# The first u and weight loads wait for relus of the opening

## The chip, the cores and the metric

The kernel runs on one core of a Trainium2 chip. Such a core has a matrix engine (TensorE, "PE" in the profile; its weight loads are "PEld"), a vector engine (VectorE, "DVE"), a scalar engine (ScalarE, "ACT"), a general engine (GpSimd, "POOL") and a fifth that mainly issues transfers (SyncE, "SP"). Each runs its own list of instructions in order, and waits on semaphores for the others. Sixteen DMA engines move data between the chip's main memory (DRAM) and the on-chip memory (SBUF); TensorE writes its results to PSUM. The metric is the device time of one execution, in microseconds; lower is better.

## The reference

Two stages follow each other, for a batch of 8 sequences of 3200 rows, with u and v 256 wide and z 64 wide:

```python
scores = scale * np.matmul(z, z.transpose(0, 2, 1))      # scale = 1 / S
attn = np.maximum(scores, 0.0) ** 2
out = np.matmul(attn, v)
x = u * out
...
wq = x @ w_q
wk = x @ w_k
W_tok = scale * np.einsum('bsd,btd->bst', wq, wk)
mixed = np.einsum('bst,btd->bsd', W_tok, x)
return np.maximum(mixed, 0.0) @ w_out
```

The first stage is most of the work: for each sequence a 3200 x 3200 matrix of scores, relu and square of it, and its product with v.

## The kernel before

**Tiles.** Rows are cut into 25 tiles of 128. The 25 tiles are put into seven groups for the output side, six of 4 tiles and one of 1. For each batch b, group gi and tile ti there is one 128 x 512 block of squared scores, and blocks are made two at a time, as a *pair*. A pair goes through four steps: TensorE makes the scores into a PSUM tile (`sc`, line 224; two such PSUM slots exist, so the scores of pair p wait for the relu of pair p-2), VectorE or ScalarE takes the relu (`g`, lines 247 and 243), GpSimd or ScalarE squares it into fp16 (`at`, lines 262 and 260), and TensorE uses the square as the stationary operand against v (`acc`, line 303). Since the matrix is symmetric, some blocks are not made again but turned by a DMA transpose on SyncE (`tt`, `ttl`, line 282). When a group's accumulators are closed, `gate` adds their two halves (`both`, lines 319 and 320) and multiplies by u (`x_sb`, line 335, on GpSimd). The second stage's matmuls (`qk`, `hd`, `mx`, `fo`) are put in between the first stage's.

**A written-out order.** The program does not leave the order to a scheduler. A planner in the kernel keeps a clock for each engine (`clock`), one for SyncE (`sp_at`) and one for the DMA engines (`dma_at`), adds an estimated duration for each instruction that it emits, and decides by these clocks what comes next on each engine. Transfers by SyncE are queued with `move(ready, due, issue, takes, fn)`; when TensorE's clock has passed `ready` and SyncE is free, `send` emits the one with the earliest `due`. The chip knows nothing of these clocks: it sees only the order of instructions on each engine, and the semaphores for the data that they share.

**The opening.** Before the loop, z of batch 0 comes in four chunks (`load_first_z`: three by SyncE, one by ScalarE), is cast to fp16 and doubled (`cast_first`, by VectorE, ScalarE and GpSimd) and turned by TensorE (`turn_first`, line 126). v of batch 0 comes in five loads, issued by GpSimd between its casts and converted to fp16 on the way (`load_first_v`, line 108): tiles 0-1, 2-3, 12-17, 18-24, 4-11. TensorE's first product with v is that of tiles 2 and 3. In the plan, `v_at` holds the time at which each tile of v is taken to be there. Then stand, as moves of SyncE, the first load of u (`load_u(0, 0)`, line 853, needed by the first gate), the second (`load_u(0, 1)`, from `group_begun`), and seven weight loads (`load_weights`, line 184; w_out first).

The plan sends the first u load when its clock for TensorE stands at 10.2, the second at 15.2, w_out at 18.1. On the chip these three read only inputs and write fresh buffers, so in the program before they have nothing to wait for.

The function `use_pair` (line 583) emits one pair's scores and relu; `first_stage` (line 239) emits the relu itself. The relu of pair p is done by VectorE for pairs 0, 3, 4, 6, 7, 9 and by ScalarE for pairs 1, 2, 5, 8.

Of the kernel before, what the change touches and what calls it, by code (L numbers as in the profile page):

```python
# [16 lines left out]
def kernel(  # L17
# [10 lines left out]
    nc = tc.nc  # L28
# [58 lines left out]
    zT, vs, us, xs, xTs, qks, ks, hacc, hx, hss, rts, zds = ({} for _ in range(12))  # L87

    def rows(t, b):
        return t[b].rearrange("(p n) d -> p n d", n=NT)  # L90
# [31 lines left out]
    def turn_first(c):  # L122
        n0, nn = ZCH[c]
        tp = acc_tile(1 - c // 2, c % 2, "ztp", FP16)
        for i in range(nn):
            nc.tensor.transpose(
                tp[:, ts(i, P)], zd0[:, n0 + i, :, :].rearrange("p a k -> p (a k)"), ident
            )
        clock[PE] += 0.14 * nn
        ready = clock[PE] + FROM_PE  # L130
        on_act = max(clock[ACT], ready) < max(clock[DVE], ready)
        copy = nc.scalar.copy if on_act else nc.vector.tensor_copy
        copy(out=zT[0][:, ds(n0 * P, nn * P)], in_=tp[:, 0 : nn * P])
        z_at[c] = give(ACT if on_act else DVE, ready, 0.2 + 0.065 * nn)
# [26 lines left out]
    def load_u(b, gi):  # L161
        n0, nn = starts[gi] // P, widths[gi] // P
        us[b, gi] = pu.tile([P, 4, D], FP32, tag="u_sb", name="u_sb")
        nc.sync.dma_start(out=us[b, gi][:, 0:nn, :], in_=rows(u, b)[:, n0 : n0 + nn, :])

# [7 lines left out]
    def load_weights():  # L175
        wo32[0] = px.tile([P, ND, D], FP32, tag="x_sb", name="wo32")
        loads = [(wo32[0][:], moe_w_out.rearrange("(c p) e -> p c e", p=P))]
        for r in range(2):
            for w32, w in ((wq32, moe_w_q), (wk32, moe_w_k)):
                loads.append((w32[top(r), :, :], w.rearrange("(c p) h -> p c h", p=dh)))  # L180
        for half in range(2):
            loads.append((wk2[:, :, half, :], moe_w_k.rearrange("(c p) h -> p c h", p=P)))
        for i, (t, w) in enumerate(loads):
            move(18.0 + i, 26.0 + i, 0.65, 0.5, lambda t=t, w=w: nc.sync.dma_start(out=t, in_=w))
# [34 lines left out]
    def scores(p):  # L219
        assert len(ztimes) >= 5 * tiles[2 * p + 1][0] and p_chunk(p) in z_at, (p, clock, len(ztimes), z_at)  # L220
        sc = ps_tile("sc")
        for h, (b, gi, ti) in enumerate(tiles[2 * p : 2 * p + 2]):
            gs, gw = starts[gi], widths[gi]
            nc.tensor.matmul(  # L224
                out=sc[:, h, 0:gw],
                lhsT=zT[b][top(h), ts(ti, P)],
                rhs=zT[b][top(h), ds(gs, gw)],
                start=True,
                stop=True,
            )  # L230
        return sc

    def pieces(p):
        ws = [widths[gi] for _, gi, _ in tiles[2 * p : 2 * p + 2]]
        if ws[0] == ws[1]:
            return [(slice(0, 2), ws[0])]
        return [(slice(h, h + 1), w) for h, w in enumerate(ws)]

    def first_stage(p, sc, on_act):
        g = pg.tile([P, 2, W], FP32, tag="g", name="g")  # L240
        for hs, w in pieces(p):
            if on_act:
                nc.scalar.activation(  # L243
                    out=g[:, hs, 0:w], in_=sc[:, hs, 0:w], func=RELU, scale=GSCALE
                )
            else:
                nc.vector.tensor_scalar(  # L247
                    out=g[:, hs, 0:w], in0=sc[:, hs, 0:w], scalar1=0.0,
                    scalar2=GSCALE, op0=AOP.max, op1=AOP.mult,
                )  # L250
        return g

    def second_stage(p, g, on_act):
        at = pat.tile([P, 2 * W], FP16, tag="at", name="at")
# [264 lines left out]
    PE, DVE, ACT, POOL = range(4)  # L519
    clock = [0.0] * 4  # L520
    FROM_PE, HOP = 0.27, 0.12

    def give(engine, ready, weight):
        clock[engine] = max(clock[engine], ready) + weight
        return clock[engine] + HOP
# [9 lines left out]
    sp_at, dma_at = [0.0], [0.0]  # L535
# [4 lines left out]
    def at_time(t, fn):  # L540
        later.append((t, fn))

    def move(ready, due, issue, takes, fn, landed=None, may=None):
        moves.append((ready, due, issue, takes, fn, landed, may))

    def send(x):
        moves.remove(x)
        _, _, issue, takes, fn, landed, _ = x
        fn()
        begun = max(sp_at[0], clock[PE])  # L550
        dma_at[0] = max(dma_at[0], begun) + takes
        sp_at[0] = max(begun + issue, dma_at[0] - RING)
        if landed:
            landed(max(sp_at[0], dma_at[0]) + LANDS)
# [5 lines left out]
    def flush():  # L560
        while True:
            ripe = [x for x in later if x[0] <= clock[PE]]
            if not ripe:
                break
            x = min(ripe, key=lambda x: x[0])
            later.remove(x)
            x[1]()
        while sp_at[0] <= clock[PE] + 0.4:
            ripe = [x for x in moves if x[0] <= clock[PE] and (not x[6] or x[6]())]
            if not ripe:  # L570
                break
            send(min(ripe, key=lambda x: x[1]))

    def open_slot():
        clock[PE] = max(clock[PE], slots.pop(0))

    def close_slot(t):
        slots.append(t)

    def cold():  # L580
        return 2.0 if clock[PE] < 11.0 else 1.0

    def use_pair():
        open_slot()
        p = produced[0]
        produced[0] += 1
        sc = scores(p)
        clock[PE] += 0.22 * cold()
        ready = clock[PE] + FROM_PE
        on_act = max(clock[ACT], ready) + BIAS < max(clock[DVE], ready)  # L590
        done = give(ACT, ready, 1.03) if on_act else give(DVE, ready, 1.2)
        g = first_stage(p, sc, on_act)
        close_slot(done)
        pending.append((done, p, g))

# [108 lines left out]
    def batch_begun(b, t):  # L704
        if b + 1 < B:
            t += 6 if b == 0 else 0
            at_time(t + 6, lambda: (load_z(b + 1), push(3.0)))
            for half in range(2):
                at_time(
                    t + 18 + 3 * half,  # L710
                    lambda half=half: (double_z(b + 1, half), give(DVE, clock[PE], 0.98)),
                )
            for i in range(5):
                move(t + 24 + 6 * i, t + 40 + 6 * i, 1.28, 1.05, lambda i=i: turn_z(b + 1, i))
            for i in range(5):
                at_time(t + 20 + 13 * i, lambda i=i: (load_v(b + 1, 5 * i, 5), push(2.5)))

    def group_begun(b, gi, t):
        if gi == 0:
            batch_begun(b, t)  # L720
        if gi + 1 < NG:
            move(max(t + 2, clock[POOL] + SLACK), t + 7, 0.55, 1.6, lambda: load_u(b, gi + 1))
        elif b + 1 < B:
            move(max(t + 2, clock[POOL] + SLACK), t + 7, 0.55, 1.6, lambda: load_u(b + 1, 0))
# [113 lines left out]
    load_first_v(18, 7)  # L838
    load_first_v(4, 8)
    clock[:] = [4.5, 4.95, 4.7, 7.8]  # L840
    v_at = [4.5] * 2 + [8.2] * 2 + [18.7] * 8 + [11.2] * 6 + [14.7] * 7
    dma_at[0] = 16.0
    turn_first(0)
    cast_first(3, [1])
    give(DVE, 0.0, 0.65)
# [1 line left out]
    current.update(b=0, gi=0, left=list(range(NT)), fresh=True)  # L847
    groups.pop(0)
    use_pair()
    use_pair()  # L850
    turn_first(2)
    turn_first(3)
    move(10.0, 14.0, 0.55, 1.6, lambda: load_u(0, 0))
    load_weights()
    at_time(38.0, cast_weights)
    group_begun(0, 0, 12.0)

    total = B * sum(NT * (w // P) for w in widths)
    done_acc = 0
# [2 lines left out]
    while groups or work or current["left"]:  # L862
# [14 lines left out]
        p = produced[0]  # L877
# [21 lines left out]
    while extras or later or moves:  # L899
        x = next((x for x in extras if x[1] == "proj"), None)  # L900
        if not x:
            ripe = [x for x in moves if not x[6] or x[6]()]
            x = min(later + extras + ripe, key=lambda x: x[0])
        clock[PE] = max(clock[PE], x[0])
        if x in later:
            later.remove(x)
            x[1]()
        elif x in moves:
            send(x)
        else:  # L910
            extras.remove(x)
            x[2]()
# [74 lines left out]
```

## Time and profile before

| | |
|---|---|
| time, median of 3 runs | 791.21 us (791.0 to 795.83) |
| the profiled execution | 790.96 us, of which the span from first to last instruction is 789.2 us |
| TensorE clock granted, mean over the span | 0.994 |
| PE, POOL, ACT, DVE busy | 97%, 78%, 70%, 61% of the span |
| HBM read and written | 59.64 MB, 26.21 MB |
| DMA rate, mean | 181 GB/s |
| u loads | 48 of 512 KB, 8 of 128 KB |
| v loads | 35 of 320 KB, and the five of the opening |

How to read the lines that follow: a line of the timeline has the start and the length of some instructions in microseconds from the span's start, the engine, the line in the code, the operation, what it writes and reads, a count, and in brackets how long the engine was idle before it and what ended that. An engine's name with a q (SPq) means its instruction queue: issuing and waiting, not computing. A line of the chain of waits has start, length and what the end of the program was waiting for in that stretch. A line of stretches has the busy time and the count of instructions of each engine in a window, then the share of the full TensorE clock that was granted, the mean busy share of the DMA engines, and GB/s.

### The profile page before, as it was taken

What the parts mean: (1) busy time and instruction counts of PE and PEld (TensorE: products, weight loads), DVE (VectorE), ACT (ScalarE), POOL (GpSimd) and SP (SyncE); (2) the same over time, 40 slices, a digit from 0 to 9 for tenths busy, and PEclk for the clock granted to TensorE, in tenths of its full rate; (3) what the DMA queues carried; (4) which work ended last, traced back from release to release, by engine and by line L of the source; (5) the groups of instructions that cost most, each with busy time, mean ns of one, the idle gap of its engine ahead of it and who ended that gap; (6) DMA issues with size and microseconds to landing.
All of it is one profiled execution on the core that took longest, in us unless ns stands there. A gap on an engine that the chain in (4) does not pass through costs nothing.

```text
span 789.2 us, 28159 instructions
## 1 busy us (share of the span) xinstructions
PE 763.2 (97%) x12373; PEld 645.7 (82%) x12373; DVE 479.4 (61%) x479; ACT 551.8 (70%) x659; POOL 612.9 (78%) x418
## 2 busy tenths in 40 slices
PE   6989999999999999999999999999999999999976
PEld 5879898887888888888788887988788888888864
DVE  5755577664685656754587635666468654675634
ACT  5766478766776677786687678866778767777624
POOL 7887799886998769877798876888789775787830
PEclk9999999999999999999999999999999999999998
DMA  7999999999999979999999999999999998899425
GB/s 192 146 172 165 177 160 179 156 225 194 204 184 189 220 164 194 152 189 216 210 162 170 187 214 199 177 151 208 193 207 165 178 225 160 183 163 194 122 56 220
DMA packets 310636, 142.57 MB, mean 181 GB/s; under 512 B 287985, under 2 KB 291953, under 8 KB 310513
## 3 DMA queue, kind: packets, MB, share of 16 engines
q1 hardware_dynamic: 303600, 124.60, 83.4%
q0 software_dynamic: 6768, 15.98, 14.8%
q8 instruction: 96, 1.57, 0.9%
q14 instruction: 28, 0.22, 0.1%
q10 hardware_dynamic: 144, 0.20, 0.1%
HBM read 59.64 MB, written 26.21 MB: 109 GB/s over the span
## 4 chain that ended last, share of the span: by engine, by line
PE 91%; DVE 3%; DMA 2%; issue 1%; ACT 1%; POOL 1%; SPq 0%; DVEq 0%; POOLq 0%; ACTq 0%
PE acc L303 66%; PE sc L224 12%; PE fo L456 6%; PE qk L366 3%; DVE g L247 2%; PE hd L393 1%; PE mx L429 1%; DVE both L320 1%; DMA v_sb<-in_v_dram 1%; DMA hx<-ha 1%; ACT both L319 1%; POOL x_sb L335 1%; DVE ha L410 0%; DMA z<-in_z_dram 0%; SPq L349 0%
## 5 line engine op out<-in xcount | busy, mean ns | idle before, releaser
L262 POOL TENSOR_TENSOR at<-g 128x1024 f16<-128x1024 f32 (+2 forms) x245 | 451.5, 1858 | 82.5 <-DVE g L247 66.5
L303 PE MATMUL acc<-v_sb,at 64*128 64x256 f16 x7312 | 499.1, 270 | 5.0 <-DVE both L320 2.5
L247 DVE TENSOR_SCALAR g<-sc 128x1024 f32<-128x1024 f32 (+2 forms) x309 | 363.9, 1197 | 153.0 <-PE sc L224 137.6
L303 PEld LDWEIGHTS <-at 64*128 64x128 f16 x7312 | 393.0, 94 | 66.8 <-issue 12.7
L260 ACT ACTIVATE at<-g 128x1024 f16<-128x1024 f32 x223 | 229.4, 1036 | 30.7 <-DVE g L247 27.2
L243 ACT ACTIVATE g<-sc 128x1024 f32<-128x1024 f32 (+1 forms) x159 | 159.2, 1003 | 60.5 <-PE sc L224 59.8
L335 POOL TENSOR_TENSOR x_sb<-both,u_sb 128x512 f16<-128x512 f32 (+1 forms) x112 | 134.4, 1207 | 64.4 <-DVE both L320 63.8
L224 PE MATMUL sc<-zT 64*128 64x512 f16 x920 | 180.2, 378 | 3.5 <-DVE g L247 3.1
L303 PE MATMUL acc<-v_sb,tt 64*128 64x256 f16 x2304 | 158.7, 269 | 0.0
L320 DVE TENSOR_TENSOR both<-acc,both 128x512 f32<-128x512 f32 (+1 forms) x104 | 69.1, 670 | 128.9 <-ACT both L319 128.4
L303 PEld LDWEIGHTS <-tt 64*128 64x128 f16 x2304 | 123.3, 94 | 11.6 <-issue 0.4
L319 ACT COPY both<-acc 128x512 f32<-128x512 f32 (+1 forms) x104 | 58.4, 566 | 65.5 <-PE acc L303 63.5
L224 PEld LDWEIGHTS <-zT 64*128 64x128 f16 x920 | 56.8, 94 | 17.6 <-issue 12.4
L484 ACT ACTIVATE fo<-fo 128x1024 f32<-128x1024 f32 (+2 forms) x50 | 44.9, 908 | 23.5 <-PE fo L456 22.1
L446 ACT ACTIVATE rt<-mx 128x1024 f16<-128x1024 f32 (+1 forms) x49 | 45.1, 931 | 22.1 <-PE mx L429 21.8
L456 PE MATMUL fo<-wo,rt 128*128 128x256 f16 x400 | 53.1, 276 | 1.2 <-ACT rt L444 0.6
L456 PEld LDWEIGHTS <-rt 128*128 128x128 f16 x400 | 35.4, 98 | 15.6 <-issue 9.6
L379 ACT CAST qk<-qk 128x512 f16<-128x512 f32 (+1 forms) x54 | 29.4, 544 | 21.6 <-PE qk L366 21.6
L366 PE MATMUL qk<-xT_sb,wqk 64*128 64x256 f16 (+1 forms) x404 | 32.2, 265 | 0.1
L366 PEld LDWEIGHTS <-wqk 64*128 64x128 f16 x416 | 22.8, 94 | 2.5 <-issue 0.5
L303 PE MATMUL acc<-v_sb,ttl 64*128 64x256 f16 x384 | 24.6, 269 | 0.0
L303 PEld LDWEIGHTS <-ttl 64*128 64x128 f16 x384 | 19.7, 94 | 3.5 <-issue 0.8
(42 smaller groups left out, 163.9 us busy)
## 6 DMA issues: line engine op xcount, KB each, us to landing
u_sb<-in_u_dram SPq DMA_DIRECT2D x48, 512.0 KB, 5.1
out_dram<-fo SPq DMA_DIRECT2D x45, 512.0 KB, 4.7
v_sb<-in_v_dram POOLq DMA_DIRECT2D x35, 320.0 KB, 6.0
zn<-in_z_dram POOLq DMA_DIRECT2D x7, 400.0 KB, 5.7
tt<-at SPq DMA_TRANSPOSE x144, 4.4
out_dram<-fo SPq DMA_DIRECT2D x6, 256.0 KB, 2.1
u_sb<-in_u_dram SPq DMA_DIRECT2D x8, 128.0 KB, 3.9
hx<-ha SPq DMA_DIRECT2D x16, 64.0 KB, 4.7
```

Source lines behind the costliest of these rows:

```text
L224: nc.tensor.matmul(out=sc[:, h, 0:gw], lhsT=zT[b][top(h), ts(ti, P)], rhs=zT[b][top(h), ds(gs, gw)], start=True, stop=True,)
L243: nc.scalar.activation(out=g[:, hs, 0:w], in_=sc[:, hs, 0:w], func=RELU, scale=GSCALE)
L247: nc.vector.tensor_scalar(out=g[:, hs, 0:w], in0=sc[:, hs, 0:w], scalar1=0.0, scalar2=GSCALE, op0=AOP.max, op1=AOP.mult,)
L260: nc.scalar.square(out=out, in_=g[:, hs, 0:w])
L262: nc.gpsimd.tensor_mul(out=out, in0=g[:, hs, 0:w], in1=g[:, hs, 0:w])
L303: nc.tensor.matmul(out=accs[half, r][:, ds((j % 2) * D, D)], lhsT=weights(b, gi, ti, j)[top(r), :], rhs=vs[b][top(r), ti, :], start=(first ...
L319: nc.scalar.copy(out=both[:, 0 : n * D], in_=accs[half, 0][:, 0 : n * D])
L320: nc.vector.tensor_add(out=both[:, 0 : n * D], in0=accs[half, 1][:, 0 : n * D], in1=both[:, 0 : n * D])
L335: nc.gpsimd.tensor_mul(out=xs[b, gi][:, 0:n, :, r, :].rearrange("p n c d -> p (n c) d"), in0=both[:, 0 : n * D].rearrange("p (m d) -> p m ...
L366: nc.tensor.matmul(out=ps[:, r, 0 : n * P], lhsT=wqk[top(r), c, :, :].rearrange("p t h -> p (t h)"), rhs=xTs[b, gi][top(r), 0:n, c, :], st ...
L446: nc.scalar.activation(out=out, in_=ps[:, 0:nr, 0 : ND * n * P], func=RELU)
L456: nc.tensor.matmul(out=banks[r][:, ds(j * D, D)], lhsT=flat[:, ds((dc * n + j) * P, P)], rhs=wo[:, dc, :], start=(dc == 0 and j == 0), sto ...
```

## The change

Two things are changed, both for the plan's first microseconds.

First, a load that SyncE sends while the planner's TensorE clock is below 32 is given one more dependency: it waits for the last relu that by the plan's clock is done at that time. Since `send` uses what the move's function returns, only functions that return their instruction take part: `load_u`, which now returns it, and the weight loads. The transposes return nothing and are as before.

Second, some of the plan's numbers are others: v is taken to land earlier (`v_at`), the DMA engines to be free at 13 rather than 16, the first u load is wanted from 13 on rather than 10, and the first group is counted as begun at 14 rather than 12, which also moves the planned times of the next batch's loads of z and v by 2.

```diff
     def load_u(b, gi):
...
-        nc.sync.dma_start(out=us[b, gi][:, 0:nn, :], in_=rows(u, b)[:, n0 : n0 + nn, :])
+        return nc.sync.dma_start(out=us[b, gi][:, 0:nn, :], in_=rows(u, b)[:, n0 : n0 + nn, :])
...
-                nc.scalar.activation(
+                relu = nc.scalar.activation(
                     out=g[:, hs, 0:w], in_=sc[:, hs, 0:w], func=RELU, scale=GSCALE
                 )
...
-        return g
+        return g, relu
...
+    SEES = mybir.DependencyInfo(mybir.DependencyClass.Sync, mybir.DependencyReason.DATA)
+    EARLY = 32.0
+    relus = []
+
     def send(x):
         moves.remove(x)
         _, _, issue, takes, fn, landed, _ = x
-        fn()
+        sent = fn()
+        if sent is not None and clock[PE] < EARLY:
+            name = [i.ins.name for t, i in relus if t <= clock[PE]][-1]
+            tc.add_manual_dep(sent.ins, name, SEES, reason="not before this relu")
         begun = max(sp_at[0], clock[PE])
...
-        g = first_stage(p, sc, on_act)
+        g, relu = first_stage(p, sc, on_act)
+        if clock[PE] < EARLY:
+            relus.append((done, relu))
...
-    v_at = [4.5] * 2 + [8.2] * 2 + [18.7] * 8 + [11.2] * 6 + [14.7] * 7
-    dma_at[0] = 16.0
+    v_at = [4.5] * 2 + [6.5] * 2 + [13.0] * 8 + [8.5] * 6 + [10.5] * 7
+    dma_at[0] = 13.0
...
-    move(10.0, 14.0, 0.55, 1.6, lambda: load_u(0, 0))
+    move(13.0, 17.0, 0.55, 1.6, lambda: load_u(0, 0))
...
-    group_begun(0, 0, 12.0)
+    group_begun(0, 0, 14.0)
```

In the built program the first u load waits for VectorE's relu of pair 4, the second for that of pair 7 and w_out for that of pair 9; the loads of w_q and w_k, which stand between transposes as before, wait for relus of pairs 10 to 19. SyncE's first 31 transfers are of the same kinds in the same order. On TensorE the order is the same through the first group, and differs from the second group on. Over the whole program GpSimd has 253 squares in place of 245, ScalarE 215 in place of 223.

More of the change, by code (lines that the diff above doesn't have):

```diff
@@ L246, in first_stage @@
             else:
-                nc.vector.tensor_scalar(
+                relu = nc.vector.tensor_scalar(
                     out=g[:, hs, 0:w], in0=sc[:, hs, 0:w], scalar1=0.0,
```

## The prediction

> **What bounds the kernel now.** I read the page first.
>
> ```profile
> span 789.2 us, 28159 instructions
> ...
> PE 763.2 (97%) x12373; PEld 645.7 (82%) x12373; DVE 479.4 (61%) x479; ACT 551.8 (70%) x659; POOL 612.9 (78%) x418
> ```
>
> TensorE is busy in all but 26 us of the span, so a change elsewhere pays only where it closes one of its gaps or keeps its clock up. Next, the chain of waits in order of time, which says where the first gap comes from:
>
> ```profile
> 0.74 2.94 DMA z<-in_z_dram
> ...
> 3.74 0.45 POOL zd L120
> 4.18 6.57 DMA v_sb<-in_v_dram
> 10.75 0.14 issue
> ```
>
> The second v load (rows 2 and 3, issued by GpSimd at 4.18) takes 6.57 us to land, and the chain runs through it. SyncE's own timeline shows what is beside it:
>
> ```profile
> 0.74 1.36 SPq L105 DMA_DIRECT2D z<-in_z_dram  x3
> 2.15 0.91 SPq L164 DMA_DIRECT2D u_sb<-in_u_dram  x2
> 3.10 0.43 SPq L184 DMA_DIRECT2D wo<-in_moe_w_out_dram  x1
> 19.15 1.35 SPq L282 DMA_TRANSPOSE tt<-at  x1
> ```
>
> Two u loads of 512 KB and w_out of 256 KB are sent by 3.53, in front of that v load, and SyncE then has nothing to do until 19.15. The stretches by DMA share and clock:
>
> ```profile
> 6.00:9.50 3.50, 2.81 (x23) 1.32 (x19) 2.37 (x4) 3.00 (x4) 2.33 (x4) 1.00 1.04 346
> 9.50:14.50 5.00, 3.62 (x34) 2.90 (x36) 2.68 (x3) 3.55 (x4) 4.46 (x3) 0.68 1.11 224
> ```
>
> ```profile
> 7.90:11.30 3.40, 1.65 (x20) 1.10 (x22) 3.05 (x4) 2.31 (x3) 3.39 (x5) 1.00 1.10 276
> 11.30:14.70 3.40, 3.40 (x32) 2.63 (x30) 1.22 (x1) 2.74 (x3) 2.86 (x2) 0.50 1.07 214
> 14.70:18.10 3.40, 3.40 (x58) 2.98 (x55) 2.35 (x2) 1.14 (x3) 2.16 (x2) 1.00 0.59 119
> ```
>
> The columns are busy time and instructions of PE, PEld, DVE, ACT, POOL, then granted clock, DMA share and GB/s. The DMA engines are full from 6 to 14.5, at 346 GB/s while u passes and 224 GB/s once v is alone. TensorE is busy 1.65 us of 3.40 in the stretch where it waits for v, and in the very next stretch its clock is granted at 0.50. The wait for v is thus paid twice: as idle time, and as half clock.
>
> **What the loads' new waits cost.** In the built program the first u load waits for the relu of pair 4, the second for that of pair 7, w_out for that of pair 9, all on VectorE. With today's trace these end at 13.26, 17.52 and 19.51:
>
> ```profile
> 7.13 0.43 DVE L120 CAST zd<-z 128x512 f16<-128x512 f32 x1 [1.56 <-DMA z<-in_z_dram]
> 7.48 1.22 DVE L247 TENSOR_SCALAR g<-sc 128x1024 f32<-128x1024 f32 x1
> ...
> 9.74 1.22 DVE L247 TENSOR_SCALAR g<-sc 128x1024 f32<-128x1024 f32 x1
> ...
> 12.04 1.22 DVE L247 TENSOR_SCALAR g<-sc 128x1024 f32<-128x1024 f32 x1 [1.08 <-PE sc L224]
> 15.17 2.35 DVE L247 TENSOR_SCALAR g<-sc 128x1024 f32<-128x1024 f32 x2 [1.91 <-PE sc L224]
> 18.29 1.22 DVE L247 TENSOR_SCALAR g<-sc 128x1024 f32<-128x1024 f32 x1 [0.77 <-PE sc L224]
> ```
>
> (The relu of pair 0 is the row at 7.48, pair 3 at 9.74, pair 4 at 12.04, pairs 6 and 7 at 15.17, pair 9 at 18.29.) Behind w_out on SyncE stands the first transpose, issued at 19.15 today; on that clock it would go at 19.51 + 0.43 = 19.94, 0.8 us late, and everything behind it by at most that. Who needs these things, and when:
>
> ```profile
> 27.99 1.27 POOL L335 TENSOR_TENSOR x_sb<-both,u_sb 128x512 f16<-128x512 f32 x1 [1.14 <-DVE both L320]
> ...
> 40.08 0.61 POOL L190 CAST wo<-wo 128x512 f16<-128x512 f32 x1
> ```
>
> ```profile
> 33.09 0.79 PE L303 MATMUL acc<-v_sb,tt 64*128 64x256 f16 x10
> ```
>
> u at 27.99, w_out at 40.08, the first turned block at 33.09. A u load issued at 13.3 that took the whole 6.57 us of the v load would land at 19.9, eight us early. I cost the waits at nothing; the cover is those eight us for u, and some seven for the transpose even if it needs 6 us to land. The small weight loads (w_q, w_k) stand where they stood, between transposes, and wait for relus that end before the transposes around them may go. If the cover went, the gate would hold the first accumulator and each us would be paid by TensorE in full.
>
> **What goes: the wait for v.** How soon v can land is not in this trace; the nearest landings are these:
>
> ```profile
> v_sb<-in_v_dram POOLq DMA_DIRECT2D x35, 320.0 KB, 6.0
> ...
> v_sb<-in_v_dram POOLq DMA_DIRECT2D x2, 128.0 KB, 6.5
> ...
> z<-in_z_dram SPq DMA_DIRECT2D x1, 224.0 KB, 3.1
> ```
>
> At best like z in the same microseconds: 4.18 + 3.1 = 7.3. At worst no sooner than now, 10.75; later than now has no cause, as nothing new moves at that time. I take it near the z row, because what is removed (1.25 MB) is most of what the DMA engines carry between 6 and 9.5. Next in line behind v is then ScalarE, which makes the weights for these matmuls:
>
> ```profile
> 6.76 1.02 ACT L243 ACTIVATE g<-sc 128x1024 f32<-128x1024 f32 x1 [0.17 <-PE sc L224]
> 7.82 1.06 ACT L260 ACTIVATE at<-g 128x1024 f16<-128x1024 f32 x1
> 9.18 1.02 ACT L243 ACTIVATE g<-sc 128x1024 f32<-128x1024 f32 x1 [0.30 <-PE sc L224]
> ```
>
> The square of pair 1 ends at 8.88, so any v before that gives the same. The last z chunk, which shares the queue with u, should land earlier as well (the DVE cast at 7.13 waited 1.56 us for it), so the relu of pair 0 and the scores of pairs 2 and 3 move up by about 0.7 us, ahead of ScalarE's next relu. TensorE's first matmuls on v then start at 8.9 in place of 10.88. After eight of them (0.44) it needs a PSUM slot that the relu of pair 2 frees: 8.88 + 1.02 = 9.90. So it goes on at 9.95 where it now goes on at 11.33.
>
> ```profile
> 10.88 0.69 PE L303 MATMUL acc<-v_sb,at 64*128 64x256 f16 x8 [1.53 <-DMA v_sb<-in_v_dram]
> ...
> 18.21 0.40 PE L224 MATMUL sc<-zT 64*128 64x512 f16 x2
> ```
>
> Between these two rows TensorE's timeline lists six pairs of scores (12 matmuls) and 72 further acc matmuls, in the same order in both programs; the order differs only from the second group on, near 30 us. At full clock their rates are in the chain's rows:
>
> ```profile
> 15.56 0.22 PE sc L224 x2
> 15.78 0.98 PE acc L303 x18
> ```
>
> 6 x 0.22 + 72 x 0.98/18 = 5.24 us. Today this takes 18.21 - 11.33 = 6.88; the 1.64 us between is half of the 3.4 us at clock 0.50. Started at 9.95 and with the clock up, the work that now begins at 18.21 begins at 15.2: 3.0 us earlier, 1.4 from the start and 1.6 from the clock. The supply of relus and squares must keep pace: stepped through with 1.22 (DVE), 1.02 and 1.06 (ACT), the slots come free 0.15 to 0.2 us before TensorE asks. (The relu of pair 3 ends near 10.1; ScalarE then squares it and does the relu of pair 5, to 12.2, and TensorE wants that slot at 9.95 + 2.41 = 12.36.) That is thin; I take 0.2 off and count **2.8 us**.
>
> [...]
>
> **What moves: everything after 30 us.** The planner's clocks start with other numbers, so its order of scores, squares and transposes changes through all later batches, with no aim. What that can be worth is bounded by the idle time there is:
>
> ```profile
> 28.00:60.00 32.00, 29.29 (x476) 26.76 (x477) 19.34 (x20) 20.74 (x25) 28.51 (x23) 1.00 1.14 166
> ```
>
> ```profile
> 60.00:160.00 100.00, 98.76 (x1661) 89.93 (x1659) 66.07 (x65) 71.43 (x86) 81.87 (x55) 1.00 1.10 172
> ...
> 660.00:760.00 100.00, 100.00 (x1685) 84.83 (x1681) 57.17 (x58) 67.98 (x84) 74.30 (x46) 1.00 0.73 149
> sum 700.00, PE 695.70 PEld 591.74 DVE 431.31 ACT 500.42 POOL 560.83; mean PE 99.39 PEld 84.53 DVE 61.62 ACT 71.49 POOL 80.12
> ```
>
> TensorE is idle 2.71 us from 28 to 60, and in the seven windows of 100 us from 60 on between 1.24 (the first) and 0.00 (the last), 4.3 in all. A fresh draw of seven such windows scatters by about 0.36 x 2.6 = 0.9 us (0.36 is the spread of even chances between 0 and 1.24); with the first stretch I allow 2 us either way and take zero.
>
> **The sum.** The profiled execution took 790.96 us, a span of 789.2 and 1.8 around it; the median of three runs, 791.21, is 0.25 above it. 790.96 - 2.8 + 0.25 = **788.4**, with 786.4 to 790.4 as its own range.
>
> **The rivals.**
>
> *v is late for its own sake* (18%). The 6.57 us may be the time from GpSimd's issue to the first bytes rather than queueing behind u; the 35 later v loads take 6.0 with no u burst in front. At half of 346 GB/s, 128 KB need 0.76 us, alone 0.38, so the removal would give 0.4 us: 790.8. For it: the 6.0 row. Against: those loads are 2.5 times larger and run beside transposes and stores. [...]
>
> *The half-clock stretch stays* (10%). A wait for the slot from 9.4 to 9.9, or a thin supply, still leaves TensorE idle enough; only the 1.4 us of the earlier start remain: 790.96 - 1.4 + 0.25 = 789.8. For it: 1.65 of 3.40 busy was enough to halve the clock; against: with the earlier start that stretch would be busy some 2.8.
>
> *The new order stalls* (14%). The worst spot today is a run of scores at the end of the third group, waiting for relus:
>
> ```profile
> 52.60 0.39 PE L224 MATMUL sc<-zT 64*128 64x512 f16 x2 [0.30 <-DVE g L247]
> ...
> 54.38 0.39 PE L224 MATMUL sc<-zT 64*128 64x512 f16 x2 [0.79 <-DVE g L247]
> ```
>
> Two of its stalls come to 1.09 us. If the new order sets up three such spots more than the old one, the 2.8 us are gone; with five, one in most batches, the time is 788.4 + 5.45 = 793.9, slower than before. For it: eight squares move from ScalarE to GpSimd, so the new order is not a copy. Against: after 60 us no window has more than 1.24 idle.
>
> **Chances and range.** 58% for the forecast. The range of 785.8 to 792.0 takes in its own range with a little more, the first two rivals, and the edge of the third; about 2 in 10 is left out. About 1% (7.9 us) is what a measurement of this kernel can tell from no change. Faster by that would need 5 us beyond the opening, more than the 4.3 us of idle time between 60 and 760: 2%. Slower by that takes ten bad spots, a quarter of the third rival: 4%. Within: 94%.
>
> **What would show it.** Right, if in the new trace no DMA from SyncE but z stands before about 11, the second v load lands before 8.9, the chain passes through ScalarE's relu and square there, the stretch at clock 0.50 between 11 and 15 is gone and the first gate on GpSimd starts near 25.2 rather than 27.99. Wrong, if v still lands after 10 us, if the half clock shows later, or if the first gate is early and the end is not: then the order behind it took it back, and TensorE's idle time by windows of 100 us would show where. If u lands after the gate wants it, the cover was wrong.

## The result, and the profile after

The changed kernel takes 798.9 us (median of 16 runs, 793.21 to 809.85); the kernel before, run beside it, takes 792.81 us (16 runs, 790.86 to 795.83). The ratio is 1.0073, with a 95% interval of 1.005 to 1.0095: slower by 0.7%, where 788.4 us had been forecast. Ratios, and the figures of the runs further down, leave out executions that took over 1.5% longer than the fastest of the same kernel (here one of the 16, at 809.85 us). The profiled execution took 800.08 us, a span of 798.3.

The page of the kernel after; its first lines, and the chain by engine and by line:

```profile
span 798.3 us, 28144 instructions
...
PE 769.0 (96%) x12373; PEld 642.0 (80%) x12373; DVE 472.6 (59%) x478; ACT 548.1 (69%) x652; POOL 624.4 (78%) x426
...
PE 87%; DMA 5%; DVE 2%; ACT 2%; issue 1%; POOL 1%; SPq 0%; POOLq 0%; DVEq 0%; ACTq 0%
```

The same line of the chain in the kernel before:

```profile
PE 91%; DVE 3%; DMA 2%; issue 1%; ACT 1%; POOL 1%; SPq 0%; DVEq 0%; POOLq 0%; ACTq 0%
```

TensorE does the same 12373 matmuls, is busy 5.8 us longer with them, and the DMA engines' share of the chain is 5% where it was 2%.

The opening did what it was meant to do. SyncE's and TensorE's timelines of the kernel after (start, length, engine and line, operation, what it writes and reads, count):

```profile
0.74 1.34 SPq L105 DMA_DIRECT2D z<-in_z_dram  x3
11.85 3.45 SPq L164 DMA_DIRECT2D u_sb<-in_u_dram  x2
16.96 0.39 SPq L184 DMA_DIRECT2D wo<-in_moe_w_out_dram  x1
17.40 1.44 SPq L282 DMA_TRANSPOSE tt<-at  x1
```

```profile
7.42 1.03 PE L126 MATMUL ztp<-ident,zd 128*128 128x128 f16 x8 [0.26 <-POOL zd L120]
8.39 1.04 PE L224 MATMUL sc<-zT 64*128 64x512 f16 x4
9.22 0.91 PE L303 MATMUL acc<-v_sb,at 64*128 64x256 f16 x8
...
15.64 0.40 PE L224 MATMUL sc<-zT 64*128 64x512 f16 x2
...
18.52 1.05 PE L303 MATMUL acc<-v_sb,at 64*128 64x256 f16 x16 [0.31 <-DMA v_sb<-in_v_dram]
```

The first u load goes at 11.85 instead of 2.15, the first product with v is at 9.22 instead of 10.88, with no wait before it, and the scores that were at 18.21 are at 15.64. The first transpose is not late but earlier (17.40; it was at 19.15). The stretches of the opening, with the granted clock as the last figure but two:

```profile
7.90:11.30 3.40, 3.27 (x31) 1.76 (x30) 3.12 (x5) 2.15 (x3) 3.39 (x3) 1.00 0.98 166
11.30:14.70 3.40, 3.40 (x62) 3.09 (x58) 2.63 (x3) 2.71 (x4) 3.40 (x3) 1.00 1.05 196
```

TensorE is busy 3.27 us of the stretch in which it was busy 1.65, and the next is granted in full instead of at 0.50: 62 instructions pass in it, where 32 did.

So the time was lost later. The sum row over the same seven stretches of 100 us from 60 to 760:

```profile
sum 700.00, PE 688.11 PEld 575.06 DVE 417.19 ACT 492.58 POOL 568.73; mean PE 98.30 PEld 82.15 DVE 59.60 ACT 70.37 POOL 81.25
```

TensorE is idle 11.9 us there, against 4.3 before. Setting the n-th TensorE instruction of both traces side by side shows where, in these two executions: from the 1600th to the 5200th the kernel after is 2.3 to 3.4 us ahead; by the 5600th it is 2.1 us behind, and from the 10400th to the 10800th it falls from 1.4 to 9.1 us behind. In this execution, then, two places make the whole loss, 4.8 and 7.7 us, less the 3 us that it was ahead.

The later one first. ScalarE's, TensorE's and SyncE's timelines there, and the stretches around it:

```profile
656.13 0.84 ACT L260 ACTIVATE at<-g 128x128 f16<-128x128 f32 x2
662.85 0.38 ACT L484 ACTIVATE fo<-fo 128x256 f32<-128x256 f32 x1 [5.88 <-DMA out_dram<-fo]
663.93 1.02 ACT L446 ACTIVATE rt<-mx 128x1024 f16<-128x1024 f32 x1 [0.70 <-PE mx L429]
```

```profile
663.29 0.61 PE L429 MATMUL mx<-qk,hs 64*128 64x256 f16 x4 [4.71 <-ACT fo L484]
```

```profile
653.50 0.53 SPq L485 DMA_DIRECT2D out_dram<-fo  x1
```

```profile
653.50 9.27 DMA out_dram<-fo
```

```profile
655.00:658.50 3.50, 3.50 (x56) 2.75 (x53) 1.46 (x3) 1.97 (x4) 2.39 (x2) 1.00 1.09 254
658.50:661.80 3.30, 0.07 (x2) 0.00 (x0) 0.65 (x1) 0.00 (x0) 1.89 (x1) 1.00 1.60 152
661.80:668.60 6.80, 5.31 (x48) 4.03 (x47) 1.22 (x1) 1.99 (x3) 1.23 (x1) 0.50 0.74 210
668.60:672.00 3.40, 3.40 (x52) 2.68 (x52) 1.23 (x1) 1.02 (x1) 1.18 (x2) 1.00 0.61 137
```

The output tile `fo` has two buffers. ScalarE is to write the small output of the seventh group into the one whose store was issued at 653.50, and that store takes 9.27 us (the fourth fence, the chain of waits; the median of such stores is 4.4). For the 5.88 us before that write ScalarE does no relu, no square and frees no PSUM slot; TensorE stands 4.71 us; and then its clock is granted at 0.50 for 6.8 us, in which 48 instructions pass where the next 3.4 us let 52 through. (The DMA share counts a packet's whole time in the stretch in which it starts, so it can exceed 1.) The wait is paid a second time, as in the opening of the kernel before.

The earlier place is of the same kind, on VectorE:

```profile
318.17 1.00 DVE L410 TENSOR_TENSOR ha<-ha 128x256 f32<-128x256 f32 x1
...
331.08 0.43 DVE L420 TENSOR_TENSOR hs<-ha,hx 128x256 f16<-128x256 f32 x1 [3.22 <-DMA hx<-ha]
331.42 2.35 DVE L247 TENSOR_SCALAR g<-sc 128x1024 f32<-128x1024 f32 x2
```

```profile
315.64 8.30 SPq L282 DMA_TRANSPOSE tt<-at  x3
324.04 1.97 SPq L415 DMA_DIRECT2D hx<-ha  x2
```

```profile
332.69 0.39 PE L224 MATMUL sc<-zT 64*128 64x512 f16 x2 [1.38 <-DVE g L247]
...
333.82 0.40 PE L429 MATMUL mx<-qk,hs 64*128 64x256 f16 x4 [0.63 <-DVE g L247]
```

```profile
331.00:334.10 3.10, 1.09 (x16) 0.60 (x14) 2.69 (x3) 0.30 (x1) 1.32 (x1) 1.00 1.23 223
334.10:337.50 3.40, 3.40 (x37) 3.00 (x34) 0.69 (x1) 3.07 (x4) 1.84 (x2) 0.50 1.03 231
```

An addition on VectorE (line 420) needs `hx`, an exchange between partitions. Its data (`ha`) was done at 319.17, but SyncE issued it only at 324.04, behind three transposes that held it for 8.30 us, and its two halves took 6.5 and 6.3 us to land. VectorE waits 3.22 us for it, two relus stand behind that, TensorE is idle 2.0 us for want of their PSUM slots, and 3.4 us at clock 0.50 follow.

### The profile page after: what moved, and what is told of

Read it like the earlier page. It is cut to its first block, busy times and chain, and to the rows that moved or that the text cites. A ratio compares the mean times of both kernels' runs of the same rounds, so it can differ in the third digit from the quotient of the medians.

```text
span 798.3 us, 28144 instructions
## 1 busy us (share of the span) xinstructions
PE 769.0 (96%) x12373; PEld 642.0 (80%) x12373; DVE 472.6 (59%) x478; ACT 548.1 (69%) x652; POOL 624.4 (78%) x426
## 3 DMA queue, kind: packets, MB, share of 16 engines
q8 instruction: 96, 1.57, 0.9%
## 4 chain that ended last, share of the span: by engine, by line
PE 87%; DMA 5%; DVE 2%; ACT 2%; issue 1%; POOL 1%; SPq 0%; POOLq 0%; DVEq 0%; ACTq 0%
PE acc L303 64%; PE sc L224 12%; PE fo L456 6%; PE qk L366 3%; DMA out_dram<-fo 2%; DVE g L247 2%; PE hd L393 2%; PE mx L429 1%; DMA v_sb<-in_v_dram 1%; DMA xT_sb<-x_sb 1%; ACT at L260 1%; ACT g L243 1%; DVE both L320 1%; DMA z<-in_z_dram 1%; POOL x_sb L335 1%
## 5 line engine op out<-in xcount | busy, mean ns | idle before, releaser
L262 POOL TENSOR_TENSOR at<-g 128x1024 f16<-128x1024 f32 (+2 forms) x253 | 463.0, 1848 | 77.4 <-DVE g L247 60.7
L260 ACT ACTIVATE at<-g 128x1024 f16<-128x1024 f32 (+2 forms) x215 | 222.3, 1040 | 26.2 <-DVE g L247 23.1
L243 ACT ACTIVATE g<-sc 128x1024 f32<-128x1024 f32 (+1 forms) x160 | 161.4, 1010 | 57.1 <-PE sc L224 56.6
L224 PE MATMUL sc<-zT 64*128 64x512 f16 x920 | 177.6, 378 | 4.1 <-DVE g L247 3.7
L429 PE MATMUL mx<-qk,hs 64*128 64x256 f16 (+1 forms) x208 | 21.2, 268 | 5.4 <-ACT fo L484 4.7
```

What stands on the lines that cost most here:

```text
L224: nc.tensor.matmul(out=sc[:, h, 0:gw], lhsT=zT[b][top(h), ts(ti, P)], rhs=zT[b][top(h), ds(gs, gw)], start=True, stop=True,)
L243: relu = nc.scalar.activation(out=g[:, hs, 0:w], in_=sc[:, hs, 0:w], func=RELU, scale=GSCALE)
L260: nc.scalar.square(out=out, in_=g[:, hs, 0:w])
L262: nc.gpsimd.tensor_mul(out=out, in0=g[:, hs, 0:w], in1=g[:, hs, 0:w])
```

## The experiments

Two parts of the change can be had apart. The waits can be put on the order of before: the loads are emitted as in the plan before, and only get the same dependencies. And the plan's numbers can be kept without the waits. Theory A was that the waits help and the new order costs; theory B, that the waits cost by what they hold up on SyncE. The runs came in three sets on three chips, each timed beside the kernel before on its own chip (medians 792.73, 792.8 and 793.1 us); the ratios are to that kernel, so runs of different sets are best compared by them.

**Waits alone** (every engine's order as before):

```diff
+    AFTER_RELU = [4, 7, 9, 10, 11, 14, 15, 19]
...
+    def release():
+        while held and held[0][0] < len(relus):
+            p, fn = held.pop(0)
+            sent = fn()
+            tc.add_manual_dep(sent.ins, relus[p].ins.name, SEES, reason="not before this relu")
...
-        fn()
+        loads = "load_u" in fn.__code__.co_freevars or "dma_start" in fn.__code__.co_names
+        if loads and AFTER_RELU:
+            held.append((AFTER_RELU.pop(0), fn))
+            release()
+        else:
+            fn()
...
+        if len(relus) < 20:
+            relus.append(relu)
+            release()
```

The plan's numbers stay those of before.

> The order of before on every engine, with the waits of after on the same relus (pairs 4, 7, 9, 10, 11, 14, 15, 19). Theory A (the waits help, the new order costs): the first product with v starts near 9.2 us, the first gate some 2 us earlier than 27.99, and the time is 2 us below before, 790.5 to 791.5 beside 792.8. Theory B (the waits themselves cost, by what they hold up on SyncE): 797 to 800, near after. If neither waits nor order alone matter, 792.8.

Measured: 789.48 us (9 runs, 787.56 to 791.74), ratio 0.9958 (0.9944 to 0.9972). Its opening and its later stretches:

```profile
24.90 1.26 POOL L335 TENSOR_TENSOR x_sb<-both,u_sb 128x512 f16<-128x512 f32 x1 [1.14 <-DVE both L320]
```

```profile
sum 700.00, PE 695.63 PEld 590.62 DVE 429.85 ACT 498.58 POOL 560.64; mean PE 99.38 PEld 84.37 DVE 61.41 ACT 71.23 POOL 80.09
```

The first gate is 3.1 us earlier (24.90; it was at 27.99), the later idle time is that of before, and the n-th TensorE instruction is 3.1 us ahead from the 400th to the 9600th. Theory A, and the opening's gain, hold; the time is 1 us below the range that theory A gave, since it counted on 2 us.

**Order alone** (`add_manual_dep` left out of the changed kernel, every engine's order as after):

> The order of after on every engine, without the waits, so u and the weights leave first as in before. Theory A: the opening as in before (first product with v at 10.9) and the later stalls as in after, so 799 to 802. Theory B: as before, 792 to 793.5.

Measured: 805.37 us (4 runs, 797.99 to 807.61), ratio 1.0143 (1.0104 to 1.0182). It is slower than the kernel after, and by more than theory A said. The order is the cause: it costs with the waits and without them. And the waits are worth even more in front of it (0.70%). The profiled execution is the fastest, so it understates the loss; it shows ScalarE waiting 7.1 us for stores in two places, near 470 and 645, neither of them the place of the kernel after.

**One number of the plan each**, without waits: `dma_at[0]` 16 to 13, and `group_begun` 12 to 14.

> Before, with one number of the plan changed (the DMA engines free at 13 in place of 16), no waits: another order from the second group on, with no aim. Theory A says that an order drawn afresh can cost several us: anything from 791 to 801, with the difference in one or two long stalls of TensorE and half-clock stretches behind them. Theory B: within 1.5 us of before.

> Before, with the other number of the plan changed (the first group begun at 14 in place of 12, which moves the next batch's loads by 2), no waits. As for the run before: theory A allows anything from 791 to 801, theory B keeps it within 1.5 us of before. If this run alone comes near after's time, it is this number that orders badly.

Measured: 790.16 us (12 runs, 786.29 to 795.92), ratio 0.9978 (0.9953 to 1.0003), and 797.49 us (11 runs, 794.06 to 803.19), ratio 1.0066 (1.0041 to 1.0091). Both numbers make another order from the second group on, and the two orders are 7 us apart; the first came out just below both theories' ranges, the second within theory A's. The new `v_at` by itself leaves the built program as it was. Without waits, the number 14 alone costs 0.66%, and all the new numbers together 1.43%; each order is a new one, so the parts don't add up to the whole.

**Is it the landings that ScalarE and VectorE wait for?** The changed kernel, with its order and waits, got the small `fo` of each seventh group a place of its own, the w_k load's tile, which has been read by then:

```diff
+        elif gi == LASTG:
+            fo = wk32
         else:
             fo = pg.tile([P, 2, W], FP32, tag="fo", name="fo", bufs=2)
```

> After, unchanged in order and waits, but the small output tile of each batch's seventh group (128 x 256) is written into the space of the w_k load, no longer used by then, in place of taking turns with the two large output tiles. ScalarE then does not stand before a store's landing at that place. Theory A1 (the order costs because ScalarE, which also makes relus and squares, waits for the landing of a store): the 5.9 us wait of ScalarE near 657, TensorE's 4.7 us behind it and the half clock of 6.8 us after it go, and the median falls from 798.9 to 791 to 795. Rival A2 (the loss is many small stalls, or the waits for relus): 797 to 800.

Measured: 793.36 us (12 runs, 790.99 to 797.91), ratio 1.0011 (0.9989 to 1.0034). ScalarE and the stretch at the place that had cost most:

```profile
656.66 0.39 ACT L486 ACTIVATE wk<-fo 128x256 f32<-128x256 f32 x1 [0.55 <-PE fo L456]
```

```profile
656.00:660.00 4.00, 4.00 (x67) 3.04 (x65) 1.96 (x2) 1.69 (x4) 2.17 (x2) 1.00 1.30 189
```

The wait of 5.88 us is 0.55 and for TensorE, and the clock stays up. This edit of one buffer takes 5.5 us off the median. Two more things stand in this trace. VectorE, which still does the addition of line 420, waits for the exchange no longer than 0.7 us, and TensorE has no gap there, so the stall near 331 was not in every execution. And TensorE now waits by itself for a transposed `x` that takes 8.71 us to land, with half clock behind it:

```profile
468.50 0.61 PE L366 MATMUL qk<-xT_sb,wqk 64*128 64x256 f16 x8 [3.00 <-DMA xT_sb<-x_sb]
```

```profile
466.08:469.49 3.41, 0.99 (x18) 0.89 (x20) 0.22 (x1) 0.34 (x1) 2.19 (x2) 1.00 1.24 230
469.49:472.90 3.41, 3.41 (x24) 1.78 (x20) 0.59 (x1) 1.27 (x2) 0.00 (x0) 0.50 1.15 344
```

Then also the addition of line 420 on GpSimd:

```diff
-            nc.vector.tensor_add(out=hss[b][:], in0=hacc.pop(b)[:, 0, :], in1=hx.pop(b)[:])
+            nc.gpsimd.tensor_add(out=hss[b][:], in0=hacc.pop(b)[:, 0, :], in1=hx.pop(b)[:])
```

> As the run before, and the addition that waits for the exchanged half of the heads (line 420) is done by GpSimd in place of VectorE, so VectorE's relus do not stand behind that transfer. Theory A1: the 3.2 us wait of VectorE near 328, TensorE's 2.0 behind it and the half clock of 3.4 go too; with both gone 789 to 792, near the run with the old order and the new waits. Rival A2: no different from the run before by more than 1 us. GpSimd's own squares may be held up by the wait instead; then the same or slower.

Measured: 789.84 us (12 runs, 786.8 to 794.36), ratio 0.9957 (0.9934 to 0.9981). Another 3.5 us; its trace has GpSimd waiting 2.8 us for that transfer, and VectorE none before the last batch. What those 3.5 us were made of no trace shows, since VectorE's wait was short in the profile of the run before. The stall near 469 is still there (2.88 us, and half clock behind it). With both edits the new order is as good as the old one with the new waits.

The same two edits on the old order with the new waits:

> The old order with the new waits (789.5), with both edits of the run before. There the profile shows neither wait, so theory A1 expects nothing or at most 1 us: 788.5 to 790.

Measured: 788.48 us (7 runs, 786.79 to 791.26), ratio 0.9939 (0.9913 to 0.9964); as expected, next to nothing: the intervals with and without them overlap. So the two edits gain 9 us in the new order and nothing clear of noise in the old one.

**Do the waits pay whatever order follows?** The new waits on the order with `dma_at[0]` at 13, and the repaired new order without them:

> The order of the run with the DMA engines free at 13 (790.2 without waits), with the waits on the same relus as after. If the waits are worth 3.1 us in the opening whatever the order behind it, as in the old order: 786.5 to 788. If the gain is lost when another order follows: 789.5 to 791.

> After with both edits (789.8), without the waits. If the waits are worth 3 us whatever follows: 792 to 794. If the order behind them hides the gain: 789 to 791.

Measured: 787.07 us (12 runs), ratio 0.9931 (0.9905 to 0.9957), where it was 0.9978 without; and 794.72 us (11 runs, 790.28 to 801.64), ratio 1.0014 (0.9987 to 1.0041), where it is 0.9957 with. The second is a little above its range. The waits are worth 0.42% in the old order, 0.47% in the one with 13 (where the intervals just touch), 0.57% in the repaired one and 0.70% in the new one as it is: 3.3 to 5.5 us. And without the waits the two edits take the new order from 1.0143 to 1.0014, some 10 us, which bears out that its loss goes with them.

**Must the loads be spread out, or is it enough that they stand behind the first v?** The old order, with u, u and w_out all behind the relu of pair 1 (`AFTER_RELU = [1, 1, 1]`; the small weight loads have no wait here):

> The old order; the two u loads and w_out all wait for the relu of pair 1 alone (about 7.4 us) and then leave together, in front of v's last three loads. If it is enough that they stand behind the first v: 789 to 790, as with the spread waits. If the spread is needed, since v's later loads are held up in their turn: TensorE waits for v between 11 and 19 us, and 790.5 to 792.5.

Measured: 791.55 us (12 runs, 789.77 to 793.67), ratio 0.9966 (0.9946 to 0.9985). SyncE sends them from 7.41 on, the first product with v is at 8.52, and then:

```profile
15.62 0.83 PE L303 MATMUL acc<-v_sb,at 64*128 64x256 f16 x12 [1.57 <-DMA v_sb<-in_v_dram]
```

TensorE waits for the fourth v load, which was issued at 7.03, ahead of them, and takes 8.5 us to land (6.8 with the waits spread out). So v is held up as the second expectation said, and the time lies in its range. That the spreading pays in time isn't shown: the interval overlaps that of the spread waits (0.9944 to 0.9972) for the most part.

**The best of both:** the order with 13, the new waits, and both edits.

> The order with the DMA engines free at 13 and the new waits (787.1), with both edits that take DMA landings out of the way of ScalarE and VectorE. Its profile shows ScalarE waiting 4.0 us for stores, with 2.1 us of TensorE and 3.4 us at half clock behind it near 655: theory A1 expects 783 to 786. If stalls of that kind only move to another place: 786 to 788.

Measured: 785.45 us (7 runs, 784.4 to 790.81), ratio 0.9909 (0.9875 to 0.9944). ScalarE's longest wait for a DMA in it is 0.5 us. Its median is the lowest of all, 7.2 us below the kernel before by the ratio; what the two edits add to the waits here is not clear of noise, as the intervals overlap (0.9905 to 0.9957 without them).

## Why the prediction was wrong

*The opening* was right in its main step, and nearly in its size. The second v load, issued at 4.20, landed 3.9 us later, at 8.1, before 8.9, and the half-clock stretch went. What came next in line was not ScalarE's square, as the prediction had it:

```profile
7.39 1.06 ACT L260 ACTIVATE at<-g 128x1024 f16<-128x1024 f32 x1
```

The square ended at 8.45; TensorE was then still at the last transposes of z (7.42), whose cast GpSimd had begun at 6.50, and at four matmuls of scores (8.39), and came to v at 9.22 in place of the forecast 8.9. 2.8 us were counted; the waits alone gave 3.1 to 3.3. In the changed kernel itself 2.6 us were left at pair 10, 0.3 went to a wait for the last v load, and the first gate started at 25.89, 2.1 us earlier than before. That last load took 10.7 us; with the waits alone, behind the same relus, it took 9.2, as in the kernel before, so the u loads don't explain the longer time.

*The waits' cost* was put at nothing, and the cover held: no gate waited for u, and the first transpose went 1.75 us earlier than before.

*"What moves: everything after 30 us"* is the step that failed. It allowed "2 us either way" and took zero, because TensorE's idle time in the old order was small. That idle time is a property of the old order: it says how much a new order can win, and nothing of what it can lose. The new order lost 9.4 us (798.9 against 789.5 with the same waits in the old order), and by the runs almost all of it goes with two edits that take DMA landings out of the way, one of ScalarE (5.5 us) and one of VectorE (3.5 us). For ScalarE the trace shows the wait and its going; for VectorE it shows the wait in one execution only. The prediction's own sign for this came: the first gate early, the end not.

*The third rival*, "the new order stalls", had the right sign and place, but its mechanism and price were those of relu waits of 1.09 us. What it lacked is that the stalls behind a DMA landing were longer (5.88 us of ScalarE behind a store that took 9.27; 3.22 us of VectorE behind an exchange that SyncE issued 4.87 us after its data was done, and that took 6.5 us to land), and that TensorE's clock was granted at 0.50 for 6.8 us after the first, which raised its price: 4.7 us of idle time cost 7.7 us. The prediction had shown that double payment in the opening, and did not carry it to the rest of the kernel.

*The first rival*, v late for its own sake, is out. As the prediction worked it out, taking u away should have saved v 0.4 us; it saved 2.6 (6.57 to 3.94). The 0.4 takes v to pass at half of 346 GB/s beside u, an estimate of the author's that no run shows. The measurement decides. The packets between 5.5 and 8.5 us show part of it; q0 is the queue of GpSimd's loads, q1 that of SyncE's (packets, MB, share of the DMA engines). Before, and after:

```profile
q1 hardware_dynamic: 276, 0.95, 88.8%
q0 software_dynamic: 37, 0.03, 6.3%
```

```profile
q0 software_dynamic: 220, 0.35, 86.7%
q1 hardware_dynamic: 8, 0.01, 1.3%
```

Beside u and w_out, GpSimd's queue got 37 packets through where it got 220 without them, so u was in its way there. Whether its packets were kept back or were queued late is not shown. (Nor was v alone from 9.5 on, as the prediction read it: w_out landed only at 14.15.)

*The second rival*, that the half clock stays, is out for the opening, and came true later, behind other waits: near 331 in the kernel after, idle times of 1.38 and 0.63 us in one stretch were followed by 3.4 us at clock 0.50, as 1.53 us were in the opening of before.

What stays open: why that store took 9.27 us. It was issued in a stretch with the DMA engines' share near 1, rising to 1.60, but which transfers held it up was not separated. Nor is it shown what the edit on VectorE saved where its wait was short, or what the order with 14 alone loses by: its trace has no wait of ScalarE for a DMA over 1 us, only half clock near 56 us behind waits of 0.89 and 1.17 us for relus.

## What to carry to other kernels

A load that is sent early because nothing holds it back can be in the way of one that is needed first (the second v load took 6.57 us to land beside u and w_out, 3.94 without); a dependency on a piece of compute, put on the load, orders the two without slowing the rest (ratio 0.9958 in the old order), and releasing all the loads at one such point made TensorE wait 1.57 us for a later part of v, which spreading them in the same order did not. In a kernel with a planned order, a change to the opening is a change to everything behind it: try the wait in the old order, and the new order without the wait, before judging either. And an instruction that waits for a DMA's landing does not belong on an engine whose other work feeds TensorE: one buffer more for the store and the addition on another engine were worth 9 us together in the new order, more than the waits themselves, though nothing clear of noise in the old one.

## What the runs showed of the hardware that was not expected

A stall of TensorE of 1.53 us was followed by half clock in the opening of before, and so were 1.38 and 0.63 us near 331 in the kernel after; 4.71 us were followed by 6.8 us of it. Other stalls of that size passed without: in the profile of the run with `dma_at[0]` at 13, idle times of 1.40 us near 413 and 1.54 near 509 left the clock at full (its mean over that execution is 0.995). Even the same stall of the same order went both ways. TensorE's idle times of 0.77 and 1.10 us near 80 left the clock up in the kernel after, and were followed by a clock of 0.50 in the run with the order alone:

```profile
74.70:78.11 3.41, 2.64 (x41) 2.19 (x38) 1.23 (x1) 1.34 (x2) 0.28 (x1) 1.00 1.52 246
78.11:81.52 3.41, 2.31 (x35) 1.70 (x33) 2.80 (x3) 3.02 (x4) 3.41 (x2) 1.00 1.07 102
81.52:84.94 3.42, 2.73 (x40) 1.96 (x38) 2.21 (x4) 3.42 (x5) 1.33 (x2) 1.00 0.86 222
```

```profile
79.18:82.59 3.41, 1.54 (x15) 0.64 (x13) 2.37 (x3) 3.35 (x4) 2.37 (x2) 1.00 1.37 184
82.59:86.00 3.41, 3.41 (x35) 2.79 (x32) 2.80 (x3) 3.05 (x5) 1.44 (x2) 0.50 0.90 167
```

In the kernel after TensorE was busy 2.64 and 2.31 us of the 3.41 around each; with the order alone both fall in the 3.41 us ahead of the half clock, with 1.54 busy. Three stretches at half clock of the kernel after, each with the 3.41 us ahead of it:

```profile
330.70:334.11 3.41, 1.40 (x22) 0.88 (x19) 2.69 (x3) 0.31 (x1) 1.33 (x1) 1.00 1.24 219
334.11:337.52 3.41, 3.41 (x36) 3.01 (x34) 0.69 (x1) 3.06 (x4) 1.83 (x2) 0.50 1.03 230
658.38:661.79 3.41, 0.19 (x4) 0.02 (x1) 0.77 (x1) 0.00 (x0) 1.89 (x1) 1.00 1.59 158
661.79:668.61 6.82, 5.32 (x48) 4.03 (x47) 1.22 (x1) 1.99 (x3) 1.24 (x1) 0.50 0.74 209
774.43:777.84 3.41, 0.26 (x1) 0.26 (x2) 0.76 (x2) 0.46 (x2) 0.00 (x0) 1.00 0.16 40
777.84:781.25 3.41, 3.41 (x14) 1.98 (x15) 0.49 (x2) 0.69 (x2) 0.00 (x0) 0.50 0.00 0
```

TensorE was busy 1.40, 0.19 and 0.26 us of 3.41 ahead of them, and 1.65 of 3.40 in the opening of before. What decides whether half clock follows is not shown. The idle times near 80 cost their own length in one execution, and 3.41 us at half clock besides in the other. The kernels with such stalls also scattered more: 793 to 805 us in the kernel after, 788 to 792 with the old order and the same waits.
